# Four low parts on VectorE move to other slots of a group, and the transpose of the attention weights moves three slots later

## The chip, the core and the metric

The kernel runs on one core of one Trainium2 chip. The metric is the device time of one execution in microseconds (us). Times of other executions are compared as medians.

## What is computed

A block of induced attention is followed by a maxout layer, over B = 4 batches of N = 12,544 tokens of C = 128 channels, with 32 inducing points and a hidden width of 768:

```python
h   = mab(I, x)          # 32 inducing points attend to all tokens of a batch
out = mab(x, h)          # every token attends to the 32 rows of h
# mab(q, kv): s = scale * q @ kv.T; s -= max; a = exp(s); a /= sum(a) + 1e-9; return a @ kv
h2  = max(out @ w1, out @ w2, out @ w3)
res = h2 @ w_out
```

## The kernel before, in words

**Groups, chunks, slots.** The 98 tiles of 128 tokens of a batch are one short group of 2 tiles and six groups of 16. A full group is four chunks of 512 tokens, and each chunk passes through six slots, one for each 128 of the hidden width. A full group is so 24 slots, the short one 6, a batch 150, the kernel 600. I call the 24 slots of a full group a window and number it b.g, batch (0 to 3) and window in the batch (0 to 5); the code's `window(6*b+g)` is its first slot. The first attention of batch 0, and the conversion of the weights, are done ahead of slot 0, in about the first 55 us.

**One slot.** The second attention and the three weight matrices are folded into `us`, so that a slot needs two matmuls on the attention weights `pT`: `pu` (L759, the difference of two of the branches) and `pv` (L765). ScalarE makes `ru` = relu of `pu` (L774), VectorE `h` = max of `pv` and `ru` (L792), the hidden values. `h` goes into the last matrix in two halves of float32r: ScalarE rounds it to `hi` (L781), and the rest, `lo` = `h` - `hi`, is made by GpSimd (L789) or, for chosen slots, by VectorE (L795). Three matmuls add them up in `acc`: `hi` with `wo_hi` (L815), `hi` with `wo_lo` (L816), `lo` with `wo_hi` (L817). The first slot of a chunk has one more (L814), and a chunk's `acc` is copied out by ScalarE (L822).

**What sets the order.** Every engine's order is written out by hand (`manual_schedule`). At step s of `main`, `advance` issues `pu` of slot s+1, `pv` of slot s, `ru` of slot s+1, `hi` of slot s-1, and `h` of slot s. GpSimd's `lo` of slot s-1 is issued there too; where the slot belongs to VectorE, its `lo` waits until the next step and stands behind that step's `h`. So a low part of slot k on VectorE is issued at step k+2, behind `h` of slot k+2, and GpSimd's of slot k+1 at the same step. Then the step's entries of `plan` are issued, and last `stage2`, the three `acc` matmuls, of slot s-6. I count steps from the window's first slot, 0 to 23. `pu` and `pv` have two PSUM banks each: `pv` of slot s+2 has to wait for `h` of slot s, `pu` of slot s+2 for `ru` of slot s. `h` has five buffers, `hi` and `lo` have ten.

**The tuples.** `LOWVEC` (L49) and `LOWLAST` (L50, for the last batch) list the slots of a window, 0 to 23, whose `lo` VectorE makes; `Chunk.low` (L805) reads them.

**The other work in a window.** `softmax2` puts the second attention's softmax of the next group at the steps of `STEPS2` (3, 5, 7, 8, 9, 10, 11, 13, 14, 15), mostly on VectorE. `turn` (L863) runs the first attention of the next batch over one group: scores on TensorE, maximum (`turn_max`, L381, VectorE), an exchange between partitions (`turn_swap`, L403, GpSimd), minimum (L411), exponentials (`turn_weights`, L418, ScalarE), sum, and `turn_transpose` (L445, VectorE), after which `turn_sums` (L459, TensorE) uses the transposed weights `aT` in a later burst. A turn starts at step 2 of a window (or at step 14 of windows 0.0 and 0.1, which hold two). Eighteen turns are spread over the windows 0.0 to 2.3. Windows 2.4 to 3.5 hold none.

Of the kernel before, what the change touches and what calls it, by code (L numbers as in the profile page):

```python
# [25 lines left out]
def kernel(ctx, tc, x, xt, ind_t, w1, w2, w3, w_out, out):  # L26
# [19 lines left out]
    ORDER = "a a a a b a a b 0 c m b a a b a b p b 1 s c b b b s S m 2 b s c 3 c s s"  # L46
    STEPS2 = (3, 5, 7, 8, 9, 10, 11, 13, 14, 15)
    scale = 1.0 / float(C) ** 0.5
    LOWVEC = (23, 0, 15, 18)  # L49
    LOWLAST = (23, 0, 9, 15, 18)  # L50
    UW = 2 * DF + C
    UQ = UW // NQ

# [743 lines left out]
    class Chunk:  # L797
# [7 lines left out]
        def low(self, k):  # L805

            return self.q is not None and NJ * self.q + k in (LOWVEC if self.b + 1 < B else LOWLAST)

# [39 lines left out]
    def at(s, f, *args):  # L848
        plan[s].append((f, args))
# [13 lines left out]
    def turn(b, k, s):  # L863

        at(s, turn_products, b, k)
        at(s + 2, turn_max, b, k)
        at(s + 3, turn_swap, b, k, 2 * M)
        at(s + 5, turn_least, b, k, False)
        at(s + 6, turn_swap, b, k, M)
        at(s + 9, turn_least, b, k, True)  # L870
        at(s + 10, turn_weights, b, k)
        at(s + 11, turn_total, b, k)
        at(s + 13, turn_transpose, b, k)

    def window(i):
        return (i // (NG - 1)) * per_batch + short + (i % (NG - 1)) * WIN
# [7 lines left out]
    for i in range(B * NW):  # L884
        b, g = i // NW, i % NW + 1
# [38 lines left out]
    for n in range(1, B):  # L924
        for k in range(NK):
            i, part = FIRST[k] if n == 1 else (NW * (n - 2) + NW - 2 + k, 0)
            turn(n, k, window(i) + BURST[part])
# [112 lines left out]
```

## Time and profile before

| | |
|---|---|
| time, median of 3 runs | 836.29 us (832.15 to 836.46) |
| the profiled execution | 836.78 us, span of its instructions 834.6 us |
| granted TensorE clock | 0.996 |
| busy TensorE (matmul) | 812.2 us, 97% of the span |
| busy ScalarE | 739.9 us, 89% |
| busy GpSimd | 665.6 us, 80% |
| busy VectorE | 651.7 us, 78% |

In the profile's rows PE is TensorE's matmul, PEld its weight load, ACT ScalarE, DVE VectorE and POOL GpSimd; L765 is line 765 of the kernel. A row of the timeline gives start and duration in us, the engine, the line and the operation, its tiles and their shapes, and how many instructions it merges; in brackets stands the idle time before it and what ended that. Matmuls overlap, so that the distance between two starts, and not the duration, is what one costs.

### The profile page before, as it was taken

To read this page: it belongs to the slowest core of one execution; us is meant where nothing else is said; L and a number is where in the kernel's file an instruction comes from. 1 tells how busy PE (TensorE), PEld (TensorE's weight loads), DVE (VectorE), ACT (ScalarE), POOL (GpSimd) and SP (SyncE) were. 2 spreads that over 40 slices of the span, in tenths; PEclk is the share of its full clock that TensorE was granted. 3 is DMA by queue.
4 is the path that set the end of the run, shared out by engine and by line. 5 is a ranking of instruction groups with operands and counts; after the bars stand their busy time and mean duration, and the time that the engine had idled before them with its cause. 6 is when DMAs were issued, how large, how long until landed. Compare 5 with 4: busy or idle time off the path is not lost.

```text
span 834.6 us, 14877 instructions
## 1 busy us (share of the span) xinstructions
PE 812.2 (97%) x4530; PEld 624.7 (75%) x4530; DVE 651.7 (78%) x1130; ACT 739.9 (89%) x1508; POOL 665.6 (80%) x632
## 2 busy tenths in 40 slices
PE   6979999999999999999999999999999999999998
PEld 4646777777777777777777777777778778778786
DVE  4967887697877888977877788779778778778864
ACT  5758898898998988988989889889899899999996
POOL 0038788797887988978979789789879888888887
PEclk9989999999999999999999999999999999999999
DMA  9415653434454334434354353333232222222221
GB/s 342 176 48 183 212 176 102 148 123 141 131 182 127 121 113 142 144 116 160 97 162 148 108 165 127 114 114 105 76 95 83 70 76 75 66 66 74 77 76 51
DMA packets 44063, 102.51 MB, mean 123 GB/s; under 512 B 9552, under 2 KB 13264, under 8 KB 38736
## 3 DMA queue, kind: packets, MB, share of 16 engines
q1 hardware_dynamic: 43984, 101.57, 38.0%
q8 instruction: 36, 0.59, 0.3%
q14 instruction: 43, 0.35, 0.1%
HBM read 48.12 MB, written 25.69 MB: 88 GB/s over the span
## 4 chain that ended last, share of the span: by engine, by line
PE 87%; DVE 5%; ACT 3%; issue 2%; POOL 1%; DMA 1%; SPq 0%; DVEq 0%; POOLq 0%; ACTq 0%
PE pv L765 16%; PE acc L815 16%; PE pu L759 15%; PE acc L816 15%; PE acc L817 15%; PE aux L678 3%; PE acc L814 3%; PE aux L362 2%; PE acc L459 2%; DVE h L792 2%; ACT ru L774 1%; ACT hi L781 1%; DMA xg<-in_x_dram 1%; POOL lo L789 1%; PE pu L269 0%
## 5 line engine op out<-in xcount | busy, mean ns | idle before, releaser
L789 POOL TENSOR_TENSOR lo<-h,hi 128x512 fp32r<-128x512 f32 (+1 forms) x498 | 638.9, 1316 | 109.1 <-ACT hi L781 59.3
L792 DVE TENSOR_TENSOR h<-pv,ru 128x512 f32<-128x512 f32 (+1 forms) x600 | 401.7, 675 | 154.9 <-PE pv L765 92.7
L774 ACT ACTIVATE ru<-pu 128x512 f32<-128x512 f32 (+1 forms) x600 | 370.3, 617 | 61.7 <-PE pu L759 57.6
L781 ACT CAST hi<-h 128x512 fp32r<-128x512 f32 (+1 forms) x600 | 379.5, 633 | 4.1 <-DVE h L792 2.7
L765 PE MATMUL pv<-pT,us 128*128 128x512 f32 (+1 forms) x600 | 235.0, 392 | 3.3 <-DVE h L792 2.1
L759 PE MATMUL pu<-pT,us 128*128 128x512 f32 (+1 forms) x600 | 234.8, 392 | 3.4 <-ACT hi L781 1.7
L815 PE MATMUL acc<-hi,wo_hi 128*128 128x512 f32 (+1 forms) x600 | 235.1, 392 | 0.0
L816 PE MATMUL acc<-hi,wo_lo 128*128 128x512 f32 (+1 forms) x600 | 231.8, 386 | 0.0
L817 PE MATMUL acc<-lo,wo_hi 128*128 128x512 f32 (+1 forms) x600 | 231.5, 386 | 0.0
L815 PEld LDWEIGHTS acc<-hi,wo_hi 128*128 128x128 f32 x600 | 112.9, 188 | 42.6 <-issue 20.7
L765 PEld LDWEIGHTS pv<-pT,us 128*128 128x128 f32 x600 | 113.3, 189 | 33.9 <-DVE h L792 12.9
L759 PEld LDWEIGHTS pu<-pT,us 128*128 128x128 f32 x600 | 113.1, 189 | 33.2 <-ACT ru L774 6.4
L817 PEld LDWEIGHTS acc<-lo,wo_hi 128*128 128x128 f32 x600 | 112.9, 188 | 23.2
L816 PEld LDWEIGHTS acc<-hi,wo_lo 128*128 128x128 f32 x600 | 113.0, 188 | 22.2
L795 DVE TENSOR_TENSOR lo<-h,hi 128x512 fp32r<-128x512 f32 x102 | 93.8, 920 | 1.8 <-ACT hi L781 1.0
L822 ACT COPY shelf<-acc 128x512 f32<-128x512 f32 (+1 forms) x100 | 60.6, 606 | 3.0 <-PE acc L817 3.0
L814 PE MATMUL acc<-pT,us 128*128 128x512 f32 (+1 forms) x100 | 39.0, 390 | 0.0
L234 POOL TENSOR_TENSOR wo_lo<-xT,wo_hi 128x768 fp32r<-128x768 f32 x1 | 1.8, 1810 | 39.6 <-ACT wo_hi L233 39.6
L678 PE MATMUL aux<-xT,hT 128*32 128x512 f32 x192 | 25.5, 604 | 0.0
L403 POOL COPY mq<-mq 32x1 f32<-32x1 f32 (+2 forms) x108 | 20.2, 187 | 5.2
L459 PEld LDWEIGHTS acc<-xg,aT 128*32 128x32 f32 x576 | 16.8, 110 | 8.5 <-issue 7.8
L814 PEld LDWEIGHTS acc<-pT,us 128*128 128x128 f32 x100 | 19.0, 190 | 3.0
(128 smaller groups left out, 451.3 us busy)
## 6 DMA issues: line engine op xcount, KB each, us to landing
out_dram<-shelf SPq DMA_DIRECT2D x96, 256.0 KB, 2.0
xg<-in_x_dram SPq DMA_DIRECT2D x23, 1024.0 KB, 5.4
xT<-in_xt_dram SPq DMA_DIRECT2D x18, 1024.0 KB, 5.1
pT<-ph SPq DMA_DIRECT2D x192, 64.0 KB, 2.0
pT<-pl SPq DMA_DIRECT2D x192, 64.0 KB, 2.0
raw<-in_w_dram SPq DMA_DIRECT2D x3, 768.0 KB, 11.7
us<-uh SPq DMA_DIRECT2D x24, 52.0 KB, 2.7
us<-ul SPq DMA_DIRECT2D x24, 52.0 KB, 1.9
```

The source lines that it names most:

```text
L759: nc.tensor.matmul(out=pu[:, :w], lhsT=state[c.b]["us"][:, 2 * j * P : (2 * j + 1) * P], rhs=c.pT[:, :w], start=True, stop=True)
L765: nc.tensor.matmul(out=pv[:, : d.w], lhsT=state[d.b]["us"][:, (2 * j + 1) * P : (2 * j + 2) * P], rhs=d.pT[:, : d.w], start=True, stop=True,)
L774: nc.scalar.activation(out=ru[:, :w], in_=pu[:, :w], func=AF.Relu)
L781: nc.scalar.copy(out=hi[:, : c.w], in_=h[:, : c.w])
L789: nc.gpsimd.tensor_sub(**args)
L792: nc.vector.tensor_max(out=h[:, : d.w], in0=pv[:, : d.w], in1=relus.pop(s)[:, : d.w])
L795: nc.vector.tensor_sub(**low)
L814: nc.tensor.matmul(out=c.acc[:, :w], lhsT=us[:, 2 * DF :], rhs=c.pT[:, :w], start=True, stop=False)
L815: nc.tensor.matmul(out=c.acc[:, :w], lhsT=wo_hi[:, j, :], rhs=c.hh[j][:, :w], start=False, stop=False)
L816: nc.tensor.matmul(out=c.acc[:, :w], lhsT=wo_lo[:, j, :], rhs=c.hh[j][:, :w], start=False, stop=False)
L817: nc.tensor.matmul(out=c.acc[:, :w], lhsT=wo_hi[:, j, :], rhs=c.hl[j][:, :w], start=False, stop=(j == NJ - 1))
L822: nc.scalar.copy(out=o[:, : c.w], in_=c.acc[:, : c.w])
```

## The change

Two tuples of slots and one offset are other numbers. The count of low parts on VectorE stays as it is, 4 in a window of the first three batches and 5 in one of the last.

```diff
-    LOWVEC = (23, 0, 15, 18)
-    LOWLAST = (23, 0, 9, 15, 18)
+    LOWVEC = (4, 8, 15, 20)
+    LOWLAST = (2, 6, 10, 15, 20)
...
-        at(s + 13, turn_transpose, b, k)
+        at(s + 16, turn_transpose, b, k)
```

Before, VectorE's low parts stand at steps 1, 2, 17 and 20 of a window (in the last batch at 11 too); after, at steps 6, 10, 17 and 22 (in the last batch at 4, 8, 12, 17 and 22). The transpose of a turn that starts at step 2 moves from step 15 to step 18; that of a turn which starts at step 14 moves from step 3 of the next window to step 6.

VectorE's order in steps 5 to 8 of window 1.2, a window with one turn, before (`mx`, `aux` are the softmax's, `mq` the turn's):

```order
L792 TENSOR_TENSOR h<-pv_75,ru 128x512
L694 TENSOR_REDUCE mx<-aux_70 128x16
L792 TENSOR_TENSOR h<-pv_74,ru 128x512
L792 TENSOR_TENSOR h<-pv_75,ru 128x512
L696 TENSOR_TENSOR aux_70<-aux_70,mx 128x512
L411 TENSOR_REDUCE mq<-mq 128x1
L792 TENSOR_TENSOR h<-pv_74,ru 128x512
```

The same steps after:

```order
L792 TENSOR_TENSOR h<-pv_75,ru 128x512
L694 TENSOR_REDUCE mx<-aux_70 128x16
L792 TENSOR_TENSOR h<-pv_74,ru 128x512
L795 TENSOR_TENSOR lo<-h,hi 128x512
L792 TENSOR_TENSOR h<-pv_75,ru 128x512
L696 TENSOR_TENSOR aux_70<-aux_70,mx 128x512
L411 TENSOR_REDUCE mq<-mq 128x1
L792 TENSOR_TENSOR h<-pv_74,ru 128x512
```

Between the `h` of slots 6 and 7 now stands the low part of slot 4.

GpSimd's order around the same steps, in a window with one turn, before (`x16` is a run of 16 rows that read alike):

```order
L789 TENSOR_TENSOR lo<-h,hi 128x512 x16
L393 COPY mq<-mm 128x1
L789 TENSOR_TENSOR lo<-h,hi 128x512
L403 COPY mq<-mq 64x1 x2
L789 TENSOR_TENSOR lo<-h,hi 128x512 x3
L403 COPY mq<-mq 32x1 x4
```

After:

```order
L789 TENSOR_TENSOR lo<-h,hi 128x512 x17
L393 COPY mq<-mm 128x1
L403 COPY mq<-mq 64x1 x2
L789 TENSOR_TENSOR lo<-h,hi 128x512 x3
L403 COPY mq<-mq 32x1 x4
```

The single low part between the two copies, that of slot 4, is gone from GpSimd, so that the next one there is that of slot 5.

VectorE's order in steps 15 to 20 of window 1.2, before:

```order
L792 TENSOR_TENSOR h<-pv_75,ru 128x512
L724 TENSOR_TENSOR pl<-aux_70,ph 128x512
L445 STREAM_TRANSPOSE aT<-a 128x512
L792 TENSOR_TENSOR h<-pv_74,ru 128x512
L792 TENSOR_TENSOR h<-pv_75,ru 128x512
L795 TENSOR_TENSOR lo<-h,hi 128x512
L792 TENSOR_TENSOR h<-pv_74,ru 128x512
L792 TENSOR_TENSOR h<-pv_75,ru 128x512
L792 TENSOR_TENSOR h<-pv_74,ru 128x512
L795 TENSOR_TENSOR lo<-h,hi 128x512
```

After:

```order
L792 TENSOR_TENSOR h<-pv_75,ru 128x512
L724 TENSOR_TENSOR pl<-aux_70,ph 128x512
L792 TENSOR_TENSOR h<-pv_74,ru 128x512
L792 TENSOR_TENSOR h<-pv_75,ru 128x512
L795 TENSOR_TENSOR lo<-h,hi 128x512
L792 TENSOR_TENSOR h<-pv_74,ru 128x512
L445 STREAM_TRANSPOSE aT<-a 128x512
L792 TENSOR_TENSOR h<-pv_75,ru 128x512
L792 TENSOR_TENSOR h<-pv_74,ru 128x512
```

The transpose has left the pair with `pl` at step 15 and stands behind the `h` of slot 18, and the low part at step 20 is gone (it is at step 22 now).

## The prediction, on record before the changed kernel was run

> **What bounds the kernel now.** I read the page first, then the list of waits, then the timeline of single windows, engine by engine. The page gives TensorE 97% of the span and 87% of the chain that ended last:
>
> ```profile
> PE 812.2 (97%) x4530; PEld 624.7 (75%) x4530; DVE 651.7 (78%) x1130; ACT 739.9 (89%) x1508; POOL 665.6 (80%) x632
> PE 87%; DVE 5%; ACT 3%; issue 2%; POOL 1%; DMA 1%; SPq 0%; DVEq 0%; POOLq 0%; ACTq 0%
> L789 POOL TENSOR_TENSOR lo<-h,hi 128x512 fp32r<-128x512 f32 (+1 forms) x498 | 638.9, 1316 | 109.1 <-ACT hi L781 59.3
> L795 DVE TENSOR_TENSOR lo<-h,hi 128x512 fp32r<-128x512 f32 x102 | 93.8, 920 | 1.8 <-ACT hi L781 1.0
> PEld pv L765 <- DVE h L792: 12.9, 32, 0.9
> PEld pu L759 <- ACT ru L774: 6.4, 20, 0.5
> ```
>
> So the change cannot touch the matmuls, only the places where TensorE is late. By the waits view VectorE's `h` holds TensorE up 32 times, ScalarE's `ru` 20 times. The edit can win at most the first kind, and it loses whatever new places of either kind it makes. The 920 ns of the low part on VectorE is a mean over very different ones:
>
> ```profile
> 328.27 1.28 POOL L789 TENSOR_TENSOR lo<-h,hi 128x512 fp32r<-128x512 f32 x1 [1.33 <-ACT hi L781]
> 328.43 1.67 DVE L795 TENSOR_TENSOR lo<-h,hi 128x512 fp32r<-128x512 f32 x1
> 703.75 0.69 DVE L795 TENSOR_TENSOR lo<-h,hi 128x512 fp32r<-128x512 f32 x1
> 703.45 0.71 ACT L781 CAST hi<-h 128x512 fp32r<-128x512 f32 x1
> 704.24 2.62 POOL L789 TENSOR_TENSOR lo<-h,hi 128x512 fp32r<-128x512 f32 x2 [0.67 <-ACT hi L781]
> ```
>
> In the first pair GpSimd's low part starts 0.16 us ahead; it ends at 329.55, and VectorE's, nominally 0.69, ends at 330.10, 0.55 behind that. In the second VectorE starts 0.49 ahead and takes 0.69, and both of GpSimd's take 2.62 together, 1.31 each. So a low part on VectorE and one on GpSimd don't run together: who starts later waits. GpSimd starts 0.08 behind the end of `hi` (704.16) where nothing is queued. That is the price list of the change: 0.69 for a low part that goes first, near 1.7 for one that comes just too late. The Trainium skill (SBUF — State Buffer, "Who interferes with whom") has it as a rule: a VectorE instruction with two SBUF inputs contends with GpSimd's reads, the order of issue decides, and the loser blocks for the whole instruction. By the rule alone a loser 0.16 behind would take 1.12 + 0.69 = 1.81; the trace has 1.67, and the trace decides. By the rule's 0.14 more for each of the 16 collisions below the sum would be 2.2 us longer.
>
> **Part 1: the low parts at steps 1 and 2 go away.** They cost nothing now, even when late, since the scores and sums of the burst stand between step 2 and step 3 on TensorE and VectorE waits there anyhow. So the gain is nothing. GpSimd's two additional ones end in the same pause.
>
> **Part 2: the low part at step 6.** This is the place that decides. Steps 5 to 7 of window 1.2 before:
>
> ```profile
> 334.99 1.29 POOL L789 TENSOR_TENSOR lo<-h,hi 128x512 fp32r<-128x512 f32 x1
> 336.35 0.40 POOL L403 COPY mq<-mq 64x1 f32<-64x1 f32 x2
> 335.10 0.61 ACT L781 CAST hi<-h 128x512 fp32r<-128x512 f32 x1
> 335.38 0.68 DVE L792 TENSOR_TENSOR h<-pv,ru 128x512 f32<-128x512 f32 x1
> 336.29 0.69 DVE L792 TENSOR_TENSOR h<-pv,ru 128x512 f32<-128x512 f32 x1 [0.23 <-POOL lo L789]
> 336.90 0.69 DVE L696 TENSOR_TENSOR aux<-aux,mx 128x512 f32<-128x512 f32 x1
> 337.10 0.61 ACT L774 ACTIVATE ru<-pu 128x512 f32<-128x512 f32 x1
> 337.59 0.62 ACT L781 CAST hi<-h 128x512 fp32r<-128x512 f32 x1
> 338.03 0.39 PE L765 MATMUL pv<-pT,us 128*128 128x512 f32 x1
> ```
>
> The 334.99 row is the `lo` of slot 4, which leaves GpSimd; the two copies then end by about 335.5, and GpSimd is free. `hi` of slot 5 ends at 335.71, so its `lo` starts at 335.79. On VectorE `h` of slot 6 starts at 335.38, and what follows an `h` starts 0.61 later (336.29 to 336.90): the new low part would start at 335.98. GpSimd is 0.19 ahead, because VectorE is behind by then (transpose, `turn_max`, maximum at steps 3 to 5) and ScalarE isn't. GpSimd ends at 335.79 + 1.29 = 337.08, VectorE's low part 0.55 later at 337.63, and `h` of slot 7, which starts some 0.07 ahead of the end of what is in front of it (336.90 against 336.98 above), runs from 337.56 to 338.25 and not from 336.29.
>
> Queued behind it: `pv` of slot 9 uses the bank and stands at 338.03; it now starts at 338.30, 0.27 late. `hi` of slot 7, which started at 337.59, starts 0.03 behind `h`, at 338.28: ScalarE's whole queue shifts by 0.69. Does ScalarE have slack to take that up?
>
> ```profile
> 344.14 0.64 ACT L774 ACTIVATE ru<-pu 128x512 f32<-128x512 f32 x1
> 344.83 0.49 PE L759 MATMUL pu<-pT,us 128*128 128x512 f32 x1
> 345.16 0.39 PE L765 MATMUL pv<-pT,us 128*128 128x512 f32 x1
> ```
>
> No: from 337.10 to 344.14 its 17 instructions stand start to start at about half a microsecond without an idle bracket, and the `ru` that ends at 344.78 is met by its `pu` at 344.83. It is the last to come there. So the 0.69 arrives on TensorE in full at step 14, with the 0.27 in it. I take 0.70 for each collision; its bounds are 0.27 (ScalarE makes it up) and 1.7 (a second collision at step 10, where with ScalarE shifted I get VectorE 0.2 us ahead, so that it costs nothing).
>
> The collision needs a VectorE that is behind at step 6, which the windows with a turn have: 0.0 to 2.3, 16 windows. In 0.1 and 0.2 the transpose of the second turn comes to step 6 as well, and its 0.63 (below) goes on top of the 0.27, with the 0.1 of a restart: 1.0 in place of 0.70. Loss: 14 x 0.70 + 2 x 1.0 = 11.8 us. Windows 2.4 and 2.5 and the last batch have no turn; there VectorE is on time and goes first, as in the 703.75 row: nothing.
>
> **Part 3: the low part at step 17, the one that leaves step 20, and the transpose.** Before, in the same window and in others (the second row of each pair of matmuls stands 0.23 behind the first where nothing is late):
>
> ```profile
> 347.42 0.70 DVE L445 STREAM_TRANSPOSE aT<-a 128x512 f32<-128x512 f32 x1
> 348.05 1.25 DVE L792 TENSOR_TENSOR h<-pv,ru 128x512 f32<-128x512 f32 x2
> 349.22 1.79 DVE L795 TENSOR_TENSOR lo<-h,hi 128x512 fp32r<-128x512 f32 x1
> 347.90 4.26 POOL L789 TENSOR_TENSOR lo<-h,hi 128x512 fp32r<-128x512 f32 x3
> 351.16 0.39 PE L759 MATMUL pu<-pT,us 128*128 128x512 f32 x1
> 351.67 0.50 PE L765 MATMUL pv<-pT,us 128*128 128x512 f32 x1
> 352.00 0.40 PE L815 MATMUL acc<-hi,wo_hi 128*128 128x512 f32 x1
> 86.91 0.39 PE L759 MATMUL pu<-pT,us 128*128 128x512 f32 x1
> 87.79 0.50 PE L765 MATMUL pv<-pT,us 128*128 128x512 f32 x1 [0.49 <-DVE h L792]
> 121.28 0.39 PE L759 MATMUL pu<-pT,us 128*128 128x512 f32 x1
> 122.11 0.50 PE L765 MATMUL pv<-pT,us 128*128 128x512 f32 x1 [0.45 <-DVE h L792]
> 290.70 0.39 PE L759 MATMUL pu<-pT,us 128*128 128x512 f32 x1
> 291.18 0.50 PE L765 MATMUL pv<-pT,us 128*128 128x512 f32 x1
> 445.55 0.39 PE L759 MATMUL pu<-pT,us 128*128 128x512 f32 x1
> 446.21 0.50 PE L765 MATMUL pv<-pT,us 128*128 128x512 f32 x1 [0.27 <-DVE h L792]
> 657.91 0.40 PE L759 MATMUL pu<-pT,us 128*128 128x512 f32 x1
> 658.89 0.50 PE L765 MATMUL pv<-pT,us 128*128 128x512 f32 x1 [0.58 <-DVE h L792]
> ```
>
> The transpose (0.63 to the next start) makes `h` late, GpSimd has a queue without a pause (three in 4.26), the low part takes 1.79, and `pv` comes 0.28 late, with 0.10 more at the next matmul. After, GpSimd has had rests at slots 4 and 8, the transpose is behind the low part, and I expect about 0.7 for it; the transpose's 0.63 at step 18 falls into a step of six matmuls (a chunk's first), 1.36 us at 0.23 each. The low part at step 22 meets a GpSimd without a queue. Its wait for `hi` is long over, and nobody needs it before step 26; `aT` is needed only at a later burst. Gains: 0.38 in each of seven like windows (0.3, 1.1 to 1.3, 2.1 to 2.3), 2.7; 0.76 in 0.0; 0.71 in 0.1, of which I keep 0.3, as the second turn's maximum still crowds step 16; 0.36 in each of 1.0 and 2.0; 0.54 in each of 0.5 and 1.5; and in 3.0, where a late low part costs 0.75 and more, 0.65, since the one at step 4 is as near a tie there as I can work out. Together 6.2 us.
>
> **Part 4: the last batch.** Low parts at steps 4, 8, 17 and 22 go first as the 703.75 row does, and in that stretch they cost nothing before either. The one at step 12 stands behind the two-piece step 11 and is a near tie with GpSimd; I take nothing, up to 0.4 in each of five windows.
>
> **The sum.** 11.8 - 6.2 = +5.6 us, on the profiled execution 836.78 to 842.4; against the median of the runs shown, 0.49 lower, 841.9.
>
> **The rivals.**
>
> *ScalarE makes it up.* A collision costs 0.27 and the 0.1 of the restart, since TensorE's own delay gives ScalarE time: 16 x 0.37 = 5.9, less 6.2: -0.3, 836.0, no change. For it: the collision's own delay of TensorE, 0.37, is time that ScalarE gets. Against it: the unbroken queue of 17. Chance 0.22.
>
> *VectorE goes first at step 6* (the other side). All that it takes is 0.19 us: if GpSimd's `lo` of slot 5 starts after 335.98 in the timeline above, because a copy or a wait in front of it is later than I work out, each low part takes 0.69, VectorE's lag at step 7 is within the bank's slack of about one microsecond, and the gains stay alone: with 0.1 and 3.0 whole, 2.7 + 0.76 + 0.71 + 0.72 + 1.08 + 1.3 = 7.3, 829.0. Against it: the 0.08 of the 704.24 row leaves little room. Chance 0.16.
>
> *The second and third low parts collide too.* At step 10 or 17 each adds 0.4 or more in most windows with a turn: +6 on the forecast, 848. Chance 0.07.
>
> That the change does nothing is excluded: the order of both engines differs in every window.
>
> **How the numbers follow.** The forecast has the rest, 0.55; its own range is 839 to 847, from losses of 0.5 to 0.9 each. A measurement of this kernel can tell 0.5%, 4.2 us, from no change, and the forecast's lower fifth falls inside that: slower 0.45 + 0.07 = 0.52, same 0.22 + 0.10 = 0.32, faster 0.16. The range, 832 to 849, leaves out most of the second rival and the tail of the third.
>
> **What would show it.** Right: in the profile after, the L795 row at step 6 of windows with a turn takes 1.6 to 1.8 with an L789 that starts 0.1 to 0.3 ahead, the next `pv` but one is about 0.3 late, and ScalarE shows an idle bracket before L781 at step 8; the L795 row at step 17 takes about 0.7, and the mean of L795 is 0.9 to 1.1. Wrong: L795 near 0.69 everywhere (the second rival), or TensorE's starts at steps 14 to 16 no later than before (the first).

## The result and the profile after

| | before | after |
|---|---|---|
| median of five runs, us | 834.92 (832.15 to 836.46) | 841.21 (840.35 to 842.86) |
| profiled execution, span, us | 836.78, 834.6 | 842.73, 841.0 |
| granted TensorE clock | 0.996 | 0.996 |
| slot 0 to the last `pu`, us | 772.07 | 777.58 |

The changed kernel is slower: ratio 1.0075, 95% interval 1.0056 to 1.0095. The page of the changed kernel, busy time, the chain of waits and the rows of the three instructions in dispute:

```profile
PE 815.9 (97%) x4530; PEld 623.3 (74%) x4530; DVE 644.8 (77%) x1130; ACT 739.1 (88%) x1508; POOL 666.3 (79%) x632
...
PE 86%; DVE 8%; issue 3%; ACT 2%; DMA 1%; POOL 0%; SPq 0%; ACTq 0%; DVEq 0%
...
L789 POOL TENSOR_TENSOR lo<-h,hi 128x512 fp32r<-128x512 f32 (+1 forms) x498 | 638.6, 1309 | 114.4 <-ACT hi L781 58.8
...
L781 ACT CAST hi<-h 128x512 fp32r<-128x512 f32 (+1 forms) x600 | 390.7, 651 | 14.0 <-DVE h L792 13.4
L795 DVE TENSOR_TENSOR lo<-h,hi 128x512 fp32r<-128x512 f32 x102 | 91.0, 892 | 0.6 <-PE pv L765 0.3
```

Read by the page alone, the edit looks good for VectorE: 7 us less busy than before, and the mean low part at 892 ns where it was 920. But its share of the chain rose from 5 to 8%. The waits of TensorE's weight loads in the changed kernel (us in total, times, longest):

```profile
PEld pv L765 <- DVE h L792: 18.9, 40, 1.2
...
PEld pu L759 <- ACT ru L774: 9.0, 22, 0.5
```

They were 12.9 and 6.4. So TensorE waits more for both engines, while both have about as much to do. The mean hides it, as in the changed kernel most low parts are clean and a few are not. Window 1.2 of the changed kernel, by the timeline; ahead of it two starts of `pu` that are one window apart, behind it three low parts of window 3.5:

```profile
328.01 0.39 PE L759 MATMUL pu<-pT,us 128*128 128x512 f32 x1
...
360.32 0.39 PE L759 MATMUL pu<-pT,us 128*128 128x512 f32 x1
...
339.72 2.99 POOL L789 TENSOR_TENSOR lo<-h,hi 128x512 fp32r<-128x512 f32 x2 [0.38 <-ACT hi L781]
...
339.22 0.68 DVE L792 TENSOR_TENSOR h<-pv,ru 128x512 f32<-128x512 f32 x1
339.82 1.75 DVE L795 TENSOR_TENSOR lo<-h,hi 128x512 fp32r<-128x512 f32 x1
341.50 0.68 DVE L792 TENSOR_TENSOR h<-pv,ru 128x512 f32<-128x512 f32 x1
...
342.21 0.62 ACT L781 CAST hi<-h 128x512 fp32r<-128x512 f32 x1 [0.66 <-DVE h L792]
...
341.65 0.39 PE L759 MATMUL pu<-pT,us 128*128 128x512 f32 x1
342.23 0.50 PE L765 MATMUL pv<-pT,us 128*128 128x512 f32 x1 [0.19 <-DVE h L792]
342.56 0.40 PE L815 MATMUL acc<-hi,wo_hi 128*128 128x512 f32 x1
...
343.26 0.40 PE L759 MATMUL pu<-pT,us 128*128 128x512 f32 x1
343.50 0.48 PE L765 MATMUL pv<-pT,us 128*128 128x512 f32 x1
343.82 0.40 PE L815 MATMUL acc<-hi,wo_hi 128*128 128x512 f32 x1
...
349.07 0.39 PE L817 MATMUL acc<-lo,wo_hi 128*128 128x512 f32 x1
349.52 0.50 PE L759 MATMUL pu<-pT,us 128*128 128x512 f32 x1
...
353.67 0.73 DVE L795 TENSOR_TENSOR lo<-h,hi 128x512 fp32r<-128x512 f32 x1
...
820.18 1.30 POOL L789 TENSOR_TENSOR lo<-h,hi 128x512 fp32r<-128x512 f32 x1 [0.38 <-ACT hi L781]
821.67 1.50 POOL L789 TENSOR_TENSOR lo<-h,hi 128x512 fp32r<-128x512 f32 x1 [0.19 <-PE pv L765]
...
820.20 1.83 DVE L795 TENSOR_TENSOR lo<-h,hi 128x512 fp32r<-128x512 f32 x1 [0.19 <-ACT hi L781]
```

GpSimd's `lo` starts at 339.72; VectorE's starts 0.10 later and takes 1.75 in place of 0.7. The `h` behind it ends at 342.18, and `hi` (after ScalarE's only idle bracket here, 0.66) and `pv` of slot 9 start right there. A matmul's start normally stands 0.23 behind the last: 341.65 to 342.23 is 0.35 too much. The next distance, 342.23 to 342.56, is 0.33, the restart. The same pair follows once more at 343.50 (0.01 and 0.09). That is 0.35 + 0.10 + 0.10, about 0.6 us, at steps 9 and 10. Further on a `pu` is 0.22 late (349.07 to 349.52), held by ScalarE's `ru`, with its own restart; counted from the window's first slot this is step 15, the place that the prediction calls step 14. The low part at step 17 is clean, 0.73.

The low part at step 6 takes 1.53 to 1.77 in all 16 windows with a turn (GpSimd starts 0.07 to 0.32 ahead), and 1.82 in 2.5 too (GpSimd 0.02 ahead). At step 10 it takes 0.67 to 0.69 everywhere. Window lengths, from the `pu` of a window's first slot to that of the next window's, and in 3.5 to the last `pu` (the two rows above, those of the second slot, are 360.32 - 328.01 = 32.31 apart, as those of the first are), in the kernel before, the changed kernel, and one run below (slot 4 given back for slot 0):

| windows | before | after | slot 0 for slot 4 |
|---|---|---|---|
| 0.0, 0.1, 0.2 | 32.35, 34.32, 32.43 | 31.43, 35.00, 33.55 | 30.76, 33.85, 32.34 |
| 0.3, 1.2, 1.3, 2.2, 2.3 | 31.94 to 31.99 | 32.26 to 32.31 | 31.46 to 31.47 |
| 0.4, 1.4 | 32.83 | 33.39, 33.37 | 32.85 |
| 0.5, 1.5 | 32.23 | 32.45 | 31.65 |
| 1.0 + 1.1, 2.0 + 2.1 | 62.27, 62.33 | 63.31, 63.19 | 61.46, 61.44 |
| 2.4, 2.5 | 31.83, 29.55 | 31.83, 29.97 | 31.83, 29.62 |
| 3.0 | 28.54 | 27.40 | 27.39 |
| 3.1 to 3.4 | 29.37 each | 29.33 each | 29.33, last 29.73 |
| 3.5 | 26.97 | 27.37 | 27.37 |

### The profile page after: what moved, and what is told of

The parts are those of the page before. It is cut to its first block, busy times and chain, and to the rows that moved or that the text cites. A ratio compares the mean times of both kernels' runs of the same rounds, so it can differ in the third digit from the quotient of the medians.

```text
span 841.0 us, 14869 instructions
## 1 busy us (share of the span) xinstructions
PE 815.9 (97%) x4530; PEld 623.3 (74%) x4530; DVE 644.8 (77%) x1130; ACT 739.1 (88%) x1508; POOL 666.3 (79%) x632
## 4 chain that ended last, share of the span: by engine, by line
PE 86%; DVE 8%; issue 3%; ACT 2%; DMA 1%; POOL 0%; SPq 0%; ACTq 0%; DVEq 0%
PE pv L765 16%; PE acc L815 15%; PE pu L759 15%; PE acc L816 14%; PE acc L817 14%; DVE h L792 4%; PE aux L678 3%; PE acc L814 3%; PE acc L459 2%; PE aux L362 2%; ACT ru L774 1%; DMA xg<-in_x_dram 1%; PE pu L269 0%; DVE mq L289 0%; DVE aT L327 0%
## 5 line engine op out<-in xcount | busy, mean ns | idle before, releaser
L789 POOL TENSOR_TENSOR lo<-h,hi 128x512 fp32r<-128x512 f32 (+1 forms) x498 | 638.6, 1309 | 114.4 <-ACT hi L781 58.8
L774 ACT ACTIVATE ru<-pu 128x512 f32<-128x512 f32 (+1 forms) x600 | 380.4, 634 | 58.4 <-PE pu L759 55.2
L781 ACT CAST hi<-h 128x512 fp32r<-128x512 f32 (+1 forms) x600 | 390.7, 651 | 14.0 <-DVE h L792 13.4
L765 PEld LDWEIGHTS pv<-pT,us 128*128 128x128 f32 x600 | 113.0, 188 | 39.8 <-DVE h L792 18.9
L795 DVE TENSOR_TENSOR lo<-h,hi 128x512 fp32r<-128x512 f32 x102 | 91.0, 892 | 0.6 <-PE pv L765 0.3
L822 ACT COPY shelf<-acc 128x512 f32<-128x512 f32 (+1 forms) x100 | 62.6, 626 | 2.7 <-PE acc L817 2.7
L814 PEld LDWEIGHTS acc<-pT,us 128*128 128x128 f32 x100 | 18.9, 189 | 3.6
## 6 DMA issues: line engine op xcount, KB each, us to landing
raw<-in_w_dram SPq DMA_DIRECT2D x3, 768.0 KB, 11.7
```

The lines of the kernel that those rows point to most:

```text
L765: nc.tensor.matmul(out=pv[:, : d.w], lhsT=state[d.b]["us"][:, (2 * j + 1) * P : (2 * j + 2) * P], rhs=d.pT[:, : d.w], start=True, stop=True,)
L774: nc.scalar.activation(out=ru[:, :w], in_=pu[:, :w], func=AF.Relu)
L781: nc.scalar.copy(out=hi[:, : c.w], in_=h[:, : c.w])
L789: nc.gpsimd.tensor_sub(**args)
L795: nc.vector.tensor_sub(**low)
L814: nc.tensor.matmul(out=c.acc[:, :w], lhsT=us[:, 2 * DF :], rhs=c.pT[:, :w], start=True, stop=False)
```

## The experiments

The theory: the low part at step 6 stands just behind GpSimd's in 16 windows, and that alone makes the kernel slower; the other parts of the edit gain. The rivals: the low parts at other steps, the transpose, or the mere amount of work in these steps. Beside the first four runs the kernel before took 835.64 us, beside the second four 834.62; each ratio is to these. Where a part is small I also give the stretch from slot 0 to the last `pu` of the profiled execution.

**The tuples alone.** The changed kernel with the transpose back in its place:

```diff
-        at(s + 16, turn_transpose, b, k)
+        at(s + 13, turn_transpose, b, k)
```

> The new slots of the low parts alone; the transpose of the attention weights stays where it was, at step 15. Theory (the loss is made at step 6, where GpSimd's low part starts ahead of VectorE's): the loss stays, about 840 to 842 us against 841.2 for the whole change and 834.9 before; the low part at step 6 takes 1.6 to 1.8 us. Rival (the transpose at its new place, step 18 or step 6, makes the loss): back to 835 or below.

Measured: 842.68 us, ratio 1.0078 (1.0063 to 1.0094). The loss is in the tuples; the rival, that the transpose at its new place makes it, falls. The transpose's move, which is all that separates this kernel from the changed one, is worth 0.8 us here by the stretch from slot 0 (778.40 to 777.58), less than the times can tell.

**The transpose alone.** The kernel before with `s + 16`:

```diff
-        at(s + 13, turn_transpose, b, k)
+        at(s + 16, turn_transpose, b, k)
```

> The transpose three slots later alone; the low parts stay in their old slots. Theory: no low part at step 6, so no loss; the transpose no longer makes the low part at step 17 late, and the 0.38 us stalls behind it go: 829 to 832 us against 834.9 before. Rival (the transpose at its new place makes the loss): 838 to 841.

Measured: 830.28 us, ratio 0.9933 (0.9919 to 0.9947), a gain of 5.4 us. So the transpose's move is worth 5.4 alone (4.9 by the stretch from slot 0, 767.14) and 0.8 beside the tuples. The timeline tells why; first the tuples alone, steps 15 to 18 of window 1.2:

```profile
352.19 0.70 DVE L445 STREAM_TRANSPOSE aT<-a 128x512 f32<-128x512 f32 x1
352.82 1.25 DVE L792 TENSOR_TENSOR h<-pv,ru 128x512 f32<-128x512 f32 x2
353.99 0.68 DVE L795 TENSOR_TENSOR lo<-h,hi 128x512 fp32r<-128x512 f32 x1
```

and the transpose alone:

```profile
344.86 0.69 DVE L792 TENSOR_TENSOR h<-pv,ru 128x512 f32<-128x512 f32 x1 [0.27 <-ACT ru L774]
345.46 0.75 DVE L795 TENSOR_TENSOR lo<-h,hi 128x512 fp32r<-128x512 f32 x1
```

Before, this low part took 1.79 here. Either half of the edit makes it clean, the tuples by a GpSimd that has caught up (by its trace GpSimd's three low parts end at 353.95, before 353.99), the transpose by an `h` that is on time. It can be saved only once.

**Slot 4 back to slot 0.** The changed kernel with one number of one tuple as before:

```diff
-    LOWVEC = (4, 8, 15, 20)
+    LOWVEC = (0, 8, 15, 20)
```

> The changed kernel with one number of one tuple different: in the first three batches VectorE makes the low part of slot 0 in place of slot 4, so that nothing stands at step 6 and one stands at step 2, ahead of the burst. Slots 8, 15, 20, the last batch and the transpose stay as changed. Theory: the loss at step 6, 0.33 to 0.7 us in each of 16 or 17 windows, goes and the gains stay: 829 to 832 us against 841.2. Rival (low parts spread over the group are worse in general, or the last batch is): 837 to 841.

Measured: 827.75 us, ratio 0.9908 (0.9893 to 0.9923). One slot of four turns a loss of 0.75% into a gain of 0.92%: this version beats both kernels, with as much work on every engine. Its chain of waits and low parts on the page, and its waits:

```profile
PE 93%; DVE 3%; ACT 2%; issue 1%; DMA 1%; POOL 0%; SPq 0%; DVEq 0%; ACTq 0%
...
L795 DVE TENSOR_TENSOR lo<-h,hi 128x512 fp32r<-128x512 f32 x102 | 86.2, 845 | 1.7 <-PE acc L817 1.2
```

```profile
PEld pu L759 <- ACT ru L774: 6.8, 24, 0.4
PEld pv L765 <- DVE h L792: 4.2, 13, 0.5
```

VectorE's share of the chain is 3% where it was 8, and its `h` holds TensorE up for 4.2 us where it did for 18.9. From slot 0 to the last `pu` this kernel takes 764.21 us, the changed one 777.58: 13.4 us in the same stretch, 0.84 for each of 16 windows.

**The same VectorE time at step 6, without GpSimd's partner.** The version above, which the recorded text calls e3, with a useless 128x512 transpose on VectorE, one input, where the low part of slot 4 had stood:

```diff
+    scrap = hp.tile([P, 512], F32, name="scrap", tag="w2h_scrap", bufs=1)
+    def fill():
+        nc.vector.transpose(out=scrap, in_=wcat[:, :512])
...
+    for i in range(2 * NW + 4):
+        at(window(i) + 6, fill)
```

> The kernel of e3 with useless work added: a 128x512 transpose of a constant on VectorE behind the max of step 6 in the 16 windows that have a turn, 0.7 us, with one SBUF input. It is the same work for VectorE at the place where the low part of slot 4 stood, but it cannot meet GpSimd. Theory (the wait for GpSimd is the price, not VectorE's load): within 1.5 us of e3. Rival (VectorE simply has too much to do at steps 3 to 11): as slow as the whole change, 839 to 842.

Measured: 829.3 us, ratio 0.9921 (0.9904 to 0.9939). The row of the 16 filler instructions in the groups by line, and the one of window 1.2 with the GpSimd row that runs beside it:

```profile
L878 DVE STREAM_TRANSPOSE scrap<-shelf 128x512 f32<-128x512 f32 x16 | 11.2, 703 | 0.0
...
330.94 1.29 POOL L789 TENSOR_TENSOR lo<-h,hi 128x512 fp32r<-128x512 f32 x1
...
331.93 0.70 DVE L878 STREAM_TRANSPOSE scrap<-shelf 128x512 f32<-128x512 f32 x1
```

The filler starts while GpSimd's low part (330.94 to 332.23) is still running, and takes its 0.70 all the same. 0.70 us of VectorE at step 6 costs 1.5 us in all by the medians and 2.5 by the stretch from slot 0 (766.70), not 13.4. So it isn't the instruction's own time that the step can't hold, but the wait in it.

**The same low part, with GpSimd later.** The changed kernel, all its slots as they are, with more work for GpSimd at step 5:

```diff
+    scrap = const.tile([P, 1], F32, name="scrap")
+    def fill():
+        for lo in range(0, P, M):
+            nc.gpsimd.tensor_copy(out=scrap[lo : lo + M], in_=eps[lo : lo + M])
...
+    for i in range(2 * NW + 4):
+        at(window(i) + 5, fill)
```

> The changed kernel with four useless 32x1 copies on GpSimd behind the two of line 403 at step 5 of the 16 windows with a turn: work is added, none removed, the output is the reference's. In the profile of the changed kernel the two 64x1 copies take 0.40 us, GpSimd is free at 339.34 of window 1.2, its low part of slot 5 starts at 339.72 and VectorE's at 339.82; four more copies at about 0.2 each (an estimate from the 0.40) free GpSimd at about 340.1, so that VectorE goes first by 0.3. Theory (the order of the two low parts at step 6 is the cost, 0.10 us decides it): the low parts at step 6 take about 0.7 us, and the time falls to 828 to 832, as with the low part at slot 0 (827.75). Rival (a low part at step 6 is late for another reason, or the cost is the amount of work on either engine): 841 or more.

Measured: 829.56 us, ratio 0.9928 (0.9910 to 0.9946). Work was added and the kernel became 11.7 us faster than the changed one by the medians, 12.6 by the stretch from slot 0. Steps 6 and 7 of window 1.2 of this run:

```profile
332.38 1.36 POOL L879 COPY scrap<-shelf 32x1 f32<-32x1 f32 x4
333.81 2.55 POOL L789 TENSOR_TENSOR lo<-h,hi 128x512 fp32r<-128x512 f32 x2
...
332.19 0.68 DVE L792 TENSOR_TENSOR h<-pv,ru 128x512 f32<-128x512 f32 x1
332.79 0.68 DVE L795 TENSOR_TENSOR lo<-h,hi 128x512 fp32r<-128x512 f32 x1
333.38 0.69 DVE L792 TENSOR_TENSOR h<-pv,ru 128x512 f32<-128x512 f32 x1
```

The copies took 1.36, not the 0.8 that I had estimated, and held GpSimd's `lo` back to 333.81. VectorE's, at 332.79, went first, took 0.68 and was over 0.34 before GpSimd's began, so that the two did not meet. This is the prediction's second rival, brought about: it names 829.0 as its time. From slot 0 it takes 764.98 us, 0.8 more than with the low part at slot 0. The copies take nothing away; they hold GpSimd back, so that the order of the two low parts at step 6 is turned, and with that nearly the whole loss is gone, 12.6 of 13.4. At step 6 every one of the 16 low parts takes 0.68 to 0.71 now. GpSimd, which has fallen behind, makes later ones longer (1.03 at step 10 and 1.28 at step 17 of window 1.2), and these cost next to nothing: the window takes 31.50 us, and 31.47 with the low part at slot 0, where the two take 0.84 and 1.10. What a wait costs depends on how much slack VectorE has at that step.

**How the wait reaches TensorE.** Two runs without ScalarE's copy of the chunk that is finished at step 12, on the changed kernel and on the version with slot 0:

```diff
-    def finish(c):
+    def finish(c, bare=False):
...
-        nc.scalar.copy(out=o[:, : c.w], in_=c.acc[:, : c.w])
+        if not bare:
+            nc.scalar.copy(out=o[:, : c.w], in_=c.acc[:, : c.w])
...
+    bare = [window(i) + 12 for i in range(1, 2 * NW + 4)]
...
-                finish(over)
+                finish(over, s in bare)
```

> The changed kernel without ScalarE's copy of the chunk that is finished at step 12, in the 15 windows with a turn but the first: those chunks of the output are not computed (an old buffer is stored). ScalarE is 0.5 us (start to start) ahead from there. Theory (VectorE's collision makes TensorE late twice: by about 0.59 us at once, steps 8 to 10, and by about 0.22 more at steps 14 and 16, through ScalarE's queue, whose stalls there are 0.53 a window in the changed kernel and 0.31 with the low part at slot 0): the stalls behind ScalarE vanish, those behind VectorE stay: 834 to 837, and the distance to the next kernel of this pair is 9 to 12 us, where it was 13.5 with the copy. First rival (the prediction's split, 0.27 at once and 0.43 through ScalarE): 832 to 834, distance about 6 to 8. Second rival (ScalarE has no part in it): the distance stays 13 to 14.

> The same copies of ScalarE left out (those chunks of the output are not computed) of the kernel with the low part at slot 0 in place of slot 4, which ran 827.75. Theory: its stalls behind ScalarE, 3.4 us by its trace, vanish: 823.5 to 826. First rival: the same for this kernel; the distance to the one before in this pair tells them apart. Second rival (ScalarE's stalls at steps 14 and 16 have nothing to do with what stands ahead of them): 827 to 829.

Measured: 836.81 us, ratio 1.0026 (1.0012 to 1.0041), and 824.98 us, ratio 0.9877 (0.9858 to 0.9897). The distance is 11.8 us, by the two intervals about 2 either way, where it was 13.5 with the copy; by the stretch from slot 0 it is 11.4 (773.64 less 762.26), where it was 13.4. That excludes the split of my prediction (6 to 8), but does not by itself tell the theory (9 to 12) from a ScalarE without a part (13 to 14). The waits and the window lengths do. The changed kernel without the copies:

```profile
PEld pv L765 <- DVE h L792: 19.0, 40, 1.2
PEld pu L759 <- ACT ru L774: 2.1, 9, 0.2
```

The version with slot 0 without them:

```profile
PEld pv L765 <- DVE h L792: 4.8, 16, 0.5
...
PEld pu L759 <- ACT ru L774: 1.5, 3, 0.8
```

The waits for `ru` fall from 9.0 and 6.8 to 2.1 and 1.5, those for `h` stay at 19 and 4 to 5. A steady window (0.3, 1.2, 1.3, 2.2, 2.3) then takes 31.80 against 31.15 on the mean, 0.49 and 0.32 less than with the copy, which is about the 0.53 and 0.31 that the stalls behind ScalarE took there (steps 14 and 16 in the expectation are 15 and 17 by the count used here). The collision costs 0.65 without ScalarE's full queue, 0.82 with it. So by these two runs about four fifths of its price reach TensorE straight through the bank of `pv`, one fifth through ScalarE.

**A tie in the last batch.** The version with slot 0, and the last batch's slot 9 as before:

```diff
-    LOWLAST = (2, 6, 10, 15, 20)
+    LOWLAST = (2, 6, 9, 15, 20)
```

> The kernel with the low part at slot 0 in place of slot 4, and in the last batch slot 9 in place of slot 10, as it was before the change. Theory (in windows 3.4 and 3.5 the low part at step 12 starts 0.02 us behind GpSimd's and takes 1.83 in place of 0.7, which makes TensorE late by 0.26 to 0.4 in each; at step 11 it goes first): 0.3 to 0.8 us below 827.75, 826.9 to 827.5, which the times alone hardly tell, and no low part above 1 us in the last batch. Rival (the last windows are late for another reason): the same stalls in 3.4 and 3.5.

Measured: 827.64 us, ratio 0.9916 (0.9899 to 0.9934), no different by its time. Window 3.5 is back at 26.97, as expected. But window 3.4 takes 29.79, and a low part of step 22 ahead of it is a slow one:

```profile
759.36 2.99 POOL L789 TENSOR_TENSOR lo<-h,hi 128x512 fp32r<-128x512 f32 x2 [0.48 <-ACT hi L781]
...
759.51 1.70 DVE L795 TENSOR_TENSOR lo<-h,hi 128x512 fp32r<-128x512 f32 x1 [0.31 <-PE pv L765]
```

That half of the expectation is a miss: "no low part above 1 us in the last batch" did not hold. Its reading of window 3.4 was wrong as well: with slot 0 the low part of step 12 there takes 0.68, and the slow one comes earlier, at step 22 of window 3.3. It stands at the same place in both runs (window 3.4 takes 29.73 with slot 0), and not in the changed kernel, which has the same slots there (29.33). Why it comes in some of these kernels' executions and not in others is open; it is worth 0.4 us.

## Why the prediction was right

The time, the sign and the place came out as forecast: 842.4 forecast for the profiled execution and 842.73 seen, 841.9 and 841.21 for the median.

*What bounds the kernel.* Held. TensorE's busy share didn't move, and all of the difference is in its late starts. The rule drawn from the Trainium skill (SBUF — State Buffer, "Who interferes with whom"), that the order of issue decides between a VectorE instruction with two SBUF inputs and GpSimd's reads, agrees with the traces: VectorE's low part takes 1.75 where GpSimd's is 0.10 ahead, and 0.68 where VectorE's goes first, as in the fifth run. By the rule alone the loser would end 0.69 behind the winner; in window 1.2, VectorE's ends at 341.57, 0.55 behind 339.72 + 1.30, as in the pair of the kernel before. In window 3.5 VectorE is 0.02 behind and takes 1.83.

*Part 1, low parts at steps 1 and 2 gain nothing by leaving.* Not tried by itself, but the traces bear it out for the windows with a turn: in window 1.3 the low part at step 2 takes 1.76 with the transpose alone and 0.68 with slot 0 for slot 4, and the window takes 31.49 and 31.47. It doesn't hold in 3.0, which has no turn (there it took 1.69 before, and the window 28.54 where it takes 27.40 after), and which the prediction counts in part 3. The run with slot 0 keeps the one at step 2 and is, with its variant in the last batch, the fastest of the kernels that do all of the work.

*Part 2, the low part at step 6.* The mechanism held in every row that the prediction named: L795 at 1.5 to 1.8 behind an L789, `pv` of slot 9 late, an idle bracket ahead of `hi`, `ru` late at what it calls step 14, and in 16 windows. The mean of all L795 is 0.892, just under the 0.9 to 1.1 that was named. GpSimd was 0.10 to 0.12 ahead in the steady windows and not 0.19, so that the second rival was nearer than I had worked out: a tenth of a microsecond would have brought it about. Two sizes were off. A collision costs 0.82 in a steady window and not 0.70: the loss over all windows was 13.4 (by the run with slot 0) where the sum has 11.8. And its split is another. I had 0.27 at once, and the rest, 0.43, through ScalarE; measured are about 0.6 at once and 0.2 through ScalarE. `pv` of slot 9 came 0.35 late and not 0.27, as GpSimd's lead was 0.09 smaller and VectorE's wait so much longer, and had a restart. `pv` of slot 10 then waited too, with a restart of its own: it needs `h` of slot 8, which stood in VectorE's late queue behind an instruction of the softmax and one of the turn (L696, L411) and by its trace started only at 342.75. The working had left both restarts and this second wait out.

*Part 3, the late steps.* The signs held, and the gain was larger: 7.9 us by the run with slot 0 (772.07 - 764.21), where the sum has 6.2. In the steady windows it is 0.5 where I had 0.38; in 0.0 it is 1.6 and not 0.76, in 3.0 1.15 and not 0.65. I had credited too little there for fear of new ties, and the new ties were elsewhere. That gain is made by two edits of which each alone saves the low part at step 17: the transpose alone gains 5.4.

*Part 4, the last batch.* "Up to 0.4 in each" was the right size: 3.5 lost 0.4 at step 12. Window 2.5, which I had put down as clean, lost 0.4 too, for VectorE was 0.02 too late.

*The sum.* +5.6 forecast; from slot 0 on +5.5, as 13.4 - 7.9. Both terms were 1.6 to 1.7 short, and that they cancelled was luck. The time ahead of slot 0, where nothing was changed, was 0.8 longer in the profiled execution.

*The rivals.* "ScalarE makes it up" falls by its price: it names 0.37 for a collision, and 0.82 was measured. In part it was right, for of the 0.43 that was to come through ScalarE only about 0.2 did. "VectorE goes first" falls for the changed kernel, and the fifth run shows that its price was right (829.0 named, 829.56 measured). "The second and third low parts collide too" falls: 0.67 to 0.69 at step 10, and at step 17 only window 0.1 has a slow one, 1.72.

## What to carry to other kernels

Where two engines share something that only one can use at a time, look at the two starts, not at the two loads: an instruction that is a tenth of a microsecond late pays for nearly the whole of the other's, and pulls the queue behind it along. Choose for such work the steps in which its engine is sure to be first by several tenths, or in which the consumer waits anyway; a little more work on the other engine at the right place can be worth more than less work. When an edit has several parts that all touch one wait, price each alone and together, since the wait can be saved only once, and a single part may turn the sign of the sum.

## What the hardware showed beside that

- A lead of 0.02 us is enough to go first: GpSimd at 820.18 against VectorE at 820.20 makes the latter 1.83.
- GpSimd waits in the same way when it is the later one, and isn't longer when it goes first. The low part that goes first at 820.18 takes 1.30. The next one starts at 821.67, while VectorE's (820.20 to 822.03) is still running, and takes 1.50. So two of them take 2.99 us from 339.72, where two take 2.55 if VectorE's is over before they start (333.81 in the run with GpSimd later).
- A small copy on GpSimd costs far more than its size: four of 32x1 took 1.36 us from the first start to the last end (0.29 each on the mean of all 64), as long as a low part of 128x512.
